# Transposing Q and K on TensorE's row halves, V products on GpSimd, and a new order: causal attention with a gated convolution on one core

## The chip, the core and the metric

The kernel runs on one core of one Trainium2 chip. The core has five engines that run side by side and meet only at semaphores: TensorE (PE: matmuls and transposes, written to the eight PSUM banks), VectorE (DVE), ScalarE (ACT: exponentials, tanh, copies), GpSimd (POOL: no PSUM access) and SyncE (SP: issues transfers). The metric is the device time of one execution in microseconds (us), lower is better.

## The reference

Eight batches, eight heads, 576 positions, head size 64; then a gated linear unit with a causal convolution of five taps over 512 channels.

```python
def _attn_ref(q, k, v, s):
    scores = np.matmul(q, k.transpose(0, 1, 3, 2)) / np.sqrt(D)
    causal = np.triu(np.ones((S, S), dtype=bool), k=1)
    cum = np.cumsum(np.maximum(s, 0.0), axis=-1)
    bias = -(cum[:, :, :, None] - cum[:, :, None, :])
    scores = np.where(causal, -1e9, scores + np.minimum(bias, 0.0))
    attn = np.exp(scores - scores.max(-1, keepdims=True))
    attn = attn / (attn.sum(-1, keepdims=True) + 1e-09)
    return np.matmul(attn, v)

def _moe_ref(x, w_val, conv_w, w_out):      # x: heads side by side, (B, S, 512)
    xp = np.concatenate([np.zeros((B, 4, D)), x], axis=1)
    gate_pre = sum(conv_w[k] * xp[:, k:k + S, :] for k in range(5))
    gate = 1.0 / (1.0 + np.exp(-gate_pre))
    return gate * (x @ w_val) @ w_out
```

Inputs and output are 32-bit floats; the kernel computes its matmuls in bfloat16.

## The kernel before

**Tiling.** Heads are taken in pairs: pair n = 4b + p is heads 2p and 2p + 1 of batch b, 32 pairs in all. For each pair Q and K are cast to bfloat16, transposed on TensorE so that the head size lies on partitions (one head on rows 0 to 63, the other on 64 to 127), and copied to a tile `QKT`. The scores are computed with keys on partitions, in three steps (`s0`, `s1`, `s2`) of 1,024 columns over two PSUM banks; each is followed by an exponential on ScalarE (`e0`, `e1`, `e2`) into a tile `P`. The last 64 by 64 block of four pairs at once is `s4` and `e4`. The decay bias goes into V: `vp` multiplies V (with a column of twos for the row sum) by the exponential `w` of the running sum of s. `av0` and `av` multiply `P` with those products for the two heads, `rec` and `nm` normalise, `xt` transposes the result back to channels, `xe` copies it to `xT`. The taps of the convolution are sums `t1` to `t4` into `gp`: a sum `t2`, `t3` or `t4` is made on VectorE straight from PSUM, or on GpSimd out of a product `p2`, `p3`, `p4` that GpSimd or ScalarE has made before. `th` is the tanh that stands for the sigmoid, `val` the matmul with w_val, `glu` their product, `out` the matmul with w_out, `oe` its copy from PSUM and `st` the store, for row blocks of two batches at a time.

**Loads.** Batch 0 is loaded pair by pair: `ld_q.0.p` and `ld_k.0.p` (128 by 512 floats each), cast by `c_q.0.p` and `c_k.0.p`. From batch 1 on, `ld_q.b` and `ld_k.b` each bring both Q and K of two pairs, and `c_q.b`, `c_k.b` cast 2,048 elements a partition. The last 64 rows of all heads come as `tails` (`ld_t`, two transfers), are transposed by `tt` in 32 bits and copied by `te`.

**Order.** Every engine works off its own list strictly in order. All lists are written out by hand in one string, `ORDER`: each word is a step with its engine (S, T, V, A, G for SyncE, TensorE, VectorE, ScalarE, GpSimd) and, behind it, the PSUM bank or buffer that it uses. `s0.9:T:4:1` is the first score step of pair 9 on TensorE in banks 4 and 5 with tile `P` 1. All loads and stores are issued by SyncE. A step on the list waits for its inputs and for its bank or buffer to come free, and all behind it on that engine wait with it.

**What the change touches.** `qk_T` (L461) makes eight transposes of 128 by 128 for a pair into one bank; `qk_evac` (L467) copies that bank's 1,024 elements a partition to `QKT`, through the helper `copy` (L348), which also makes the casts and the `xe` and `oe` copies. `vprime` (L447) is `vp`, on GpSimd or VectorE as the list says. `mask` (L527, `mk`) sets the scores above the diagonal to zero on GpSimd; a pair without `mk` has them pushed down by two more matmuls instead (`future`, L483). `unread` (L555, `wu`) is a matmul of 512 columns whose result nobody reads. In the trace, L475 is a score matmul, L464 a Q/K transpose, L523 an exponential, L540 attention times V, L562 `xt`, L588 a tap sum on GpSimd, L575 a tap product on GpSimd and L573 one on ScalarE.

The transposes and copies in question:

```python
    def qk_T(e, b, p, *w):
        for c, which in enumerate(w or range(2)):
            for j in range(4):
                pe.transpose(bank16[:, at["qt", b, p, *w][0], c * 512 + j * 128:c * 512 + (j + 1) * 128],
                             qk_src(which, b, p, j if w else 4 * c + j), ident)
```

Of the kernel before, what the change touches and what calls it, by code (L numbers as in the profile page):

```python
# [177 lines left out]
ld_q.0.0:S wu.0:T:0 ld_s:S wu.1:T:7 ld_k.0.0:S wu.2:T:0 wu.3:T:7 ld_k.0.1:S wu.4:T:0 ld_t.0:S wu.5:T:7 wu.6:T:0  # L178
wu.7:T:7 ld_cw:S c_q.0.0:G wu.8:T:0 relu:V ld_q.0.2:S wu.9:T:7 scan:V wu.10:T:0 ld_q.0.1:S wu.11:T:7 wu.12:T:0
wu.13:T:7 ld_q.0.3:S wu.14:T:0 c_k.0.1:A wu.15:T:7 c_k.0.0:V wu.16:T:0 ld_k.0.2:S wu.17:T:7 centre:V wu.18:T:0  # L180
wu.19:T:7 ld_v.0.0:S wu.20:T:2 tt.0:T:0 qt.0.0.q:T:1 qt.0.0.k:T:2 qe.0.0.q:V cwT:T:3 qe.0.0.k:A wu.21:T:7 te.0:V
wu.22:T:6 ld_k.0.3:S s0.0:T:4:0 cwc:V s1.0:T:0 ld_v.0.1:S e0.0:A decT:T:2 qt.0.1.k:T:6 c_q.0.1:V wu.23:T:7 e1.0:A
qe.0.1.k:V mk.0:G qt.0.1.q:T:3 s2.0:T:4 qe.0.1.q:V wu.24:T:6 ld_q.1.0:S:0 e2.0:A wu.25:T:7 c_k.0.2:V c_q.0.3:G
s0.1:T:0:1 c_q.0.2:V qt.0.3.q:T:3 expw:A ld_k.1.0:S:2 s4.0.0:T:4 qe.0.3.q:V qt.0.2.q:T:6 vp.0.0:G e4.0.0:A
qt.0.2.k:T:7 e0.1:A qe.0.2.q:V s1.1:T:2 s4.0.1:T:4 qe.0.2.k:V ld_k.1.1:S wu.26:T:6 e1.1:A c_k.0.3:G av0.0:T:0 s2.1:T:6
e4.0.1:A ld_q.1.1:S s0.2:T:2:0 vp.0.1:V e2.1:A av.0:T s2.2:T:4 rec.0:V e0.2:A av0.1:T:6 ld_v.0.2:S nm.0:V av.1:T
c_q.1.0:G:0 e2.2:A qt.0.3.k:T:2 rec.1:V xt.0:T:3 qe.0.3.k:V mk.2:G qt.1.0:T:0 xe.0:A nm.1:V ld_v.0.3:S s1.2:T:4
qe.1.0:A wu.27:T:1 c_k.1.0:G:1 t1.0:V:0 xt.1:T:2 s0.3:T:6:1 e1.2:A xe.1:V s4.0.3:T:0 c_k.1.1:G t2.0:V ld_t.1:S e0.3:A
s4.0.2:T:4 t1.1:V:1 p2.1:G:0 e4.0.2:A ld_v.1.2:S t3.0:V e4.0.3:A s1.3:T:6 s2.3:T:4 e1.3:A c_q.1.1:G ld_v.1.4:S
qt.1.3:T:0 t4.1:V qt.1.2:T:1 ld_v.1.0:S e2.3:A t4.0:V s0.4:T:6:2 vp.0.2:G ld_v.1.3:S qe.1.2:V e0.4:A qt.1.1:T:3  # L190
ld_v.1.1:S av0.2:T:4 ld_wv:S:0 vp.0.3:G qe.1.3:A t3.1:V av.2:T ld_q.2:S:2 s0.6:T:6:0 rec.2:V e0.6:A nm.2:V t2.1:G
tt.1:T:2 av0.3:T:0 ld_t.2:S qe.1.1:V xt.2:T:4 te.1:A av.3:T xe.2:A mk.6:G s2.4:T:6 ld_k.2:S:1 rec.3:V th.1:A:0
s0.5:T:2:1 nm.3:V p3.2:G:0 e2.4:A t1.2:V:1 ld_wo:S:3 xt.3:T:5 s2.5:T:0 e0.5:A xe.3:V ld_v.2.3:S s1.6:T:6 t3.2:G
t1.3:V:2 ld_v.2.2:S e1.6:A s1.4:T:2 ld_v.2.4:S t2.3:V p4.2:G:1 e2.5:A s1.5:T:6 ld_v.2.0:S t2.2:V ld_v.2.1:S e1.4:A
vp.1.0:G s4.1.3:T:0 t3.3:V ld_k.3:S:4 wu.28:T:4 wu.29:T:4 e4.1.3:A s2.6:T:2 vp.1.1:V wu.30:T:4 e1.5:A t4.2:G av0.4:T:0
av.4:T t4.3:V e2.6:A av0.5:T:6 vp.1.2:V av.5:T th.3:A:1 cast_wv:G s0.7:T:2:1 rec.5:V rec.4:V th.0:A:2 av0.6:T:4 nm.5:V
av.6:T e0.7:A nm.4:V xt.5:T:6 vp.1.3:G ld_q.3:S:0 wu.31:T:7 xe.5:A rec.6:V s1.7:T:2 nm.6:V val.1.0:T:0 e1.7:A
# [544 lines left out]
```

## Time and profile before

| what | value |
|---|---|
| median of 3 runs | 194.74 us (194.48 to 195.73) |
| profiled execution, whole | 193.35 us |
| its span, first to last instruction | 191.6 us |
| mean granted TensorE clock | 0.989 |
| busy TensorE / VectorE / ScalarE / GpSimd | 176.6 / 172.9 / 166.2 / 166.8 us |
| DMA, mean over the span | 211 GB/s, 40.43 MB |

All views come from one execution, recorded by the hardware profiler. Busy time counts an engine while an instruction runs on it. The end of a matmul is modelled, so starts are the safer reading for TensorE. The chain of waits goes back from the last instruction to whatever released each step, and so says on whom the end depended. "Idle before" in a group of instructions is the time that the engine stood still ahead of them, with what ended it. An engine's idle time costs something only where the chain passes through it.

### The profile page before, as it was taken

To read this page: it belongs to the slowest core of one execution; us is meant where nothing else is said; L and a number is where in the kernel's file an instruction comes from. 1 tells how busy PE (TensorE), PEld (TensorE's weight loads), DVE (VectorE), ACT (ScalarE), POOL (GpSimd) and SP (SyncE) were. 2 spreads that over 40 slices of the span, in tenths; PEclk is the share of its full clock that TensorE was granted. 3 is DMA by queue.
4 is the path that set the end of the run, shared out by engine and by line. 5 is a ranking of instruction groups with operands and counts; after the bars stand their busy time and mean duration, and the time that the engine had idled before them with its cause. 6 is when DMAs were issued, how large, how long until landed. Compare 5 with 4: busy or idle time off the path is not lost.

```text
span 191.6 us, 6160 instructions
## 1 busy us (share of the span) xinstructions
PE 176.6 (92%) x2481; PEld 119.3 (62%) x2481; DVE 172.9 (90%) x279; ACT 166.2 (87%) x214; POOL 166.8 (87%) x136
## 2 busy tenths in 40 slices
PE   6999796899998999999997899999999999989991
PEld 2457483578556846677755577675756764757740
DVE  5597999889989799998999999999999899999973
ACT  2179999979999699989899989999999999898930
POOL 6036989998999989999999999999999999998910
PEclk9999999699999999999999999999999999999999
DMA  5998999999999997999999999279550005200515
GB/s 149 269 258 305 255 185 288 317 335 239 238 298 292 192 260 285 307 399 189 194 192 314 363 344 216 107 249 254 139 159 29 29 5 201 76 2 3 221 74 207
DMA packets 62281, 40.43 MB, mean 211 GB/s; under 512 B 47333, under 2 KB 49381, under 8 KB 62250
## 3 DMA queue, kind: packets, MB, share of 16 engines
q1 hardware_dynamic: 62250, 40.01, 76.9%
q8 instruction: 20, 0.33, 0.7%
q14 instruction: 11, 0.09, 0.2%
HBM read 30.57 MB, written 9.44 MB: 209 GB/s over the span
## 4 chain that ended last, share of the span: by engine, by line
PE 33%; DVE 21%; ACT 21%; POOL 10%; issue 9%; DMA 3%; SPq 1%; DVEq 0%; ACTq 0%; POOLq 0%
ACT P L523 9%; PE bank L540 9%; PE bank L623 6%; POOL gp L588 5%; PE bank L475 5%; PE bank L606 5%; DVE gp L586 4%; PE bank L464 3%; DVE xn L549 3%; ACT QKT L348 3%; DVE QKT L348 3%; DVE glu L614 3%; ACT th L598 3%; DMA tail<-in_k_dram 3%; POOL pr L575 2%
## 5 line engine op out<-in xcount | busy, mean ns | idle before, releaser
L523 ACT ACTIVATE P<-bank 128x1024 bf16<-128x1024 f32 x96 | 94.5, 1039 | 4.0 <-PE bank L475 2.4
L588 POOL TENSOR_TENSOR gp<-gp,pr 128x572 f32<-128x572 f32 (+2 forms) x38 | 56.2, 1486 | 3.7 <-ACT pr L573 0.9
L586 DVE SCALAR_TENSOR_TENSOR gp<-bank,cwr,gp 128x574 f32<-128x574 bf16 (+2 forms) x58 | 46.1, 802 | 0.6
L475 PE MATMUL bank<-QKT 64*128 64x128 bf16 (+4 forms) x576 | 38.0, 241 | 5.1 <-ACT P L523 2.8
L606 PE MATMUL bank<-xT,wv 128*128 128x288 bf16 x256 | 36.1, 286 | 2.1 <-DVE xT L348 0.6
L540 PE MATMUL bank<-Vp,P 128*128 128x65 bf16 x960 | 35.9, 194 | 0.7 <-ACT P L523 0.5
L540 PEld LDWEIGHTS <-P 128*128 128x128 bf16 x960 | 33.4, 98 | 4.6 <-issue 2.5
L623 PE MATMUL bank<-wo,glu 128*128 128x512 bf16 x144 | 35.3, 380 | 0.1
L575 POOL TENSOR_TENSOR pr<-xT,cwr 128x572 f32<-128x572 bf16 (+2 forms) x28 | 32.7, 1175 | 1.4 <-DVE xT L348 0.8
L475 PEld LDWEIGHTS <-QKT 64*128 64x128 bf16 x576 | 18.5, 94 | 21.8 <-issue 14.8
L606 PEld LDWEIGHTS <-wv 128*128 128x128 bf16 x256 | 23.8, 97 | 10.7 <-issue 3.4
L448 POOL TENSOR_TENSOR Vp<-vst,w 128x650 bf16<-128x650 f32 x22 | 29.0, 1335 | 0.5 <-ACT w L369 0.5
L598 ACT ACTIVATE th<-gp,cwr 128x576 f32<-128x576 f32 (+1 forms) x33 | 25.2, 780 | 3.1 <-POOL gp L588 1.9
L584 DVE SCALAR_TENSOR_TENSOR gp<-xT,cwr,bank 128x576 f32<-128x576 bf16 x32 | 25.7, 809 | 1.3 <-ACT xT L348 0.2
L549 DVE TENSOR_TENSOR xn<-bank,recs 128x640 bf16<-128x640 f32 x32 | 26.0, 819 | 0.6
L348 ACT COPY QKT<-bank 128x1024 bf16<-128x1024 bf16 (+1 forms) x25 | 24.9, 1014 | 1.8 <-PE bank L464 1.8
L614 DVE SCALAR_TENSOR_TENSOR glu<-th,bank 128x576 bf16<-128x576 f32 (+1 forms) x33 | 23.9, 731 | 2.5 <-ACT th L598 1.1
L529 POOL TENSOR_SCALAR_AFFINE_SELECT P<-P 128x1024 bf16<-128x1024 bf16 x16 | 17.5, 1094 | 8.8 <-ACT P L523 8.8
L623 PEld LDWEIGHTS <-glu 128*128 128x128 bf16 x144 | 12.5, 97 | 14.0 <-issue 2.3
L464 PE MATMUL bank<-ident,qkb 128*128 128x128 bf16 x256 | 19.3, 219 | 0.3 <-DVE gp L586 0.3
L464 PEld LDWEIGHTS <-qkb 128*128 128x128 bf16 x256 | 15.4, 98 | 3.5 <-issue 1.6
L348 POOL CAST qkb<-first 128x2048 bf16<-128x2048 f32 (+2 forms) x11 | 15.5, 1410 | 0.8 <-DMA first<-in_k_dram 0.4
(61 smaller groups left out, 182.7 us busy)
## 6 DMA issues: line engine op xcount, KB each, us to landing
out_dram<-ot SPq DMA_DIRECT2D x36, 256.0 KB, 3.1
...
```

The costliest lines, as they stand in the source:

```text
L348: (act.copy if e is act else e.tensor_copy)(dst, src)
L464: pe.transpose(bank16[:, at["qt", b, p, *w][0], c * 512 + j * 128:c * 512 + (j + 1) * 128], qk_src(which, b, p, j if w else 4 * c + j), ident)
L475: pe.matmul(ps[:, hh, c0:c0 + nq], QKTs[b % 2][r, 1, p, k0:k0 + 128], QKTs[b % 2][r, 0, p, q0:q0 + nq], **kw)
L523: act.activation(out=Pt(n)[:, :, step * 512:(step + 1) * 512], in_=pair((f"s{step}", n)), func=AF.Exp, scale=0.125)
L540: pe.matmul(ps[:, qb * 65:qb * 65 + 65], lhsT, Vps[b % 2][:, kb, 2 * p + hh, :], start=(kb == 0), stop=(kb == qb))
L549: vec.tensor_tensor(xns[b % 2][:, :, p * 128:(p + 1) * 128].rearrange("t g (w d) -> t w g d", w=2), pair(("av", n))[:, :, 0:325].rearrange ...
L575: pool.tensor_tensor(pr, xTs[b % 2][:, c, 4:4 + S - m], r.to_broadcast([128, S - m]), ALU.mult)
L586: vec.scalar_tensor_tensor(gp[:, m:S], xps(n)[:, 0:S - m], r, gp[:, m:S], ALU.mult, ALU.add)
L588: pool.tensor_tensor(gp[:, m:S], gp[:, m:S], prs[at[f"p{m}", n][0]][:, m:S], ALU.add)
L598: act.activation(out=thof(n)[:, r], in_=gps[at["t1", n][0]].rearrange("p (h s) -> p h s", h=2)[:, r], func=AF.Tanh, scale=cwr[:, n % 4, 4:5])
L606: pe.matmul(ps, wv[:, dc, c * 128:(c + 1) * 128], xTs[b % 2][:, dc, 4 + o:4 + o + 288], start=(dc == 0), stop=(dc == 3))
L623: pe.matmul(bank_of(u, i), glu2[:, c, i * 128:i * 128 + 128], wo[:, c, :], start=(c == 0), stop=(c == 3))
```

## The change

Four things change in the code, and the whole order is another one.

1. From batch 1 on (the second batch), a step `qq.b.h` takes the place of two steps `qt`: it transposes two pairs in halves. Each 128 by 128 transpose becomes two of 64 rows by 128 columns, one from TensorE's rows 0 to 63 and one from rows 64 to 127, written to two different banks. Each bank then holds half of both pairs, and `qk_evac` reads both banks for a pair. 28 of the 32 pairs go this way; batch 0 keeps `qt`.
2. All 32 `vp` are on GpSimd (22 before; ten were on VectorE).
3. Loads are issued by the engine that the list names. Six of batch 0's eight Q and K loads go out from ScalarE's queue, the rest stay on SyncE's.
4. `tt` and `te` can use two banks; no step of the new list does.

```diff
-            sync.dma_start(out=first[part][which],
+            e.dma_start(out=first[part][which],
                            in_=(q, k)[which][0, HP[part], 0:512, :].rearrange("h (p j) d -> p h (j d)", j=4))
...
+        if ("qq", b, p // 2) in at:
+            copy(e, QKTs[b % 2][:, :, p, 0:512].rearrange("d w (r x j) -> d w r x j", r=2, j=8),
+                 both_rows(b, p).rearrange("d r (j x w) -> d w r x j", w=2, j=8))
+            return
...
+    def half_T(out, src, r):
+        return pe.transpose(out, src[64 * r:64 * r + 64, :], ident[64 * r:64 * r + 64, 64 * r:64 * r + 64])
+
+    def both_rows(b, p):
+        lo, hi = sorted(at["qq", b, p // 2])
+        return bank16[:, lo:hi + 1:hi - lo, p % 2 * 512:p % 2 * 512 + 512]
+
+    def qk_T2(e, b, h):
+        for p in range(2):
+            for j in range(8):
+                for r in range(2):
+                    half_T(both_rows(b, 2 * h + p)[:, r, j * 64:j * 64 + 64], qk_src(None, b, 2 * h + p, j), r)
```

The list begins like this, before and after (SyncE, ScalarE, GpSimd, VectorE; TensorE without the `wu`):

```diff
-S ld_q.0.0 ld_s ld_k.0.0 ld_k.0.1 ld_t.0 ld_cw ld_q.0.2 ld_q.0.1 ld_q.0.3 ld_k.0.2 ld_v.0.0 ld_k.0.3
+S ld_q.0.0 ld_t.0 ld_q.0.1 ld_s ld_cw ld_v.0.0 ld_v.0.1 ld_k.1.0 ld_k.1.1 ld_q.1.0 ld_v.0.2 ld_q.1.1
-A c_k.0.1 qe.0.0.k e0.0 e1.0 e2.0 expw e4.0.0 e0.1 e1.1 e4.0.1 e2.1
+A ld_k.0.0 ld_k.0.1 ld_k.0.2 ld_q.0.2 ld_k.0.3 ld_q.0.3 c_q.0.0 qe.0.0.k e0.0 e1.0 e2.0 qe.0.2.k e0.1 e1.1 e2.1 expw
-G c_q.0.0 mk.0 c_q.0.3 vp.0.0 c_k.0.3 c_q.1.0 mk.2 c_k.1.0
+G c_k.0.0 c_k.0.1 c_q.0.1 mk.0 c_q.0.2 c_k.0.3 mk.1 vp.0.0 vp.0.1 c_k.1.0 mk.2 c_k.1.1
-V relu scan c_k.0.0 centre qe.0.0.q te.0 cwc c_q.0.1 qe.0.1.k qe.0.1.q
+V qe.0.0.q te.0 qe.0.1.k c_k.0.2 relu qe.0.1.q scan centre qe.0.2.q
-T tt.0 qt.0.0.q qt.0.0.k cwT s0.0 s1.0 decT qt.0.1.k qt.0.1.q s2.0
+T qt.0.0.k qt.0.0.q tt.0 s0.0 qt.0.1.k s1.0 qt.0.1.q s2.0 qt.0.2.k s1.1 s0.1
```

Where the new list has other numbers of steps:

| step | before | after |
|---|---|---|
| Q/K transposes | 36 `qt` | 8 `qt`, 14 `qq` |
| `vp` on GpSimd / VectorE | 22 / 10 | 32 / 0 |
| `mk` on GpSimd | 16 | 19 |
| tap sums `t2` to `t4` on GpSimd / VectorE | 38 / 58 | 35 / 61 |
| tap products on GpSimd / ScalarE | 28 / 10 | 23 / 12 |
| `oe` on ScalarE / VectorE | 20 / 16 | 23 / 13 |
| `xe` on ScalarE / VectorE | 11 / 21 | 9 / 23 |
| `qe` on ScalarE / VectorE | 25 / 11 | 26 / 10 |
| Q/K casts on GpSimd / VectorE / ScalarE | 18 / 5 / 1 | 20 / 2 / 2 |
| `wu` | 33 | 43 |

Of the casts, `c_k.5` (2,048 elements) moves from VectorE to GpSimd and `c_k.2` (2,048 elements) from GpSimd to ScalarE. The count of `wu` up to `av.6` rises by twelve. TensorE's list has 130 places before and 146 after where work on all 128 rows follows work on row halves, or the other way round.

More of the change, by code (lines that the diff above doesn't have):

```diff
@@ L177 @@
 ORDER = """
[L178 to L197, printed above, removed]
```

200 lines of the change are left out of this document (116 added, 84 removed).

## Prediction

> **What bounds the kernel now.** I read the page first: its chain of waits says which engine the end hangs on.
>
> ```profile
> span 191.6 us, 6160 instructions
> ...
> PE 33%; DVE 21%; ACT 21%; POOL 10%; issue 9%; DMA 3%; SPq 1%; DVEq 0%; ACTq 0%; POOLq 0%
> ACT P L523 9%; PE bank L540 9%; PE bank L623 6%; POOL gp L588 5%; PE bank L475 5%; PE bank L606 5%; DVE gp L586 4%; PE bank L464 3%; DVE xn L549 3%; ACT QKT L348 3%; DVE QKT L348 3%; DVE glu L614 3%; ACT th L598 3%; DMA tail<-in_k_dram 3%; POOL pr L575 2%
> ```
>
> No engine owns the chain: it changes hands between four. So I cut the span into stages with the view of busy time by windows (busy us of PE, weight loads, DVE, ACT, POOL; then TensorE's granted clock, DMA share, GB/s).
>
> ```profile
> 0.00:20.00 20.00, 18.17 (x199) 10.54 (x199) 13.79 (x35) 10.95 (x15) 9.05 (x19) 1.00 0.93 250
> 20.00:42.00 22.00, 18.58 (x321) 12.60 (x320) 20.71 (x32) 20.48 (x27) 20.78 (x17) 0.92 1.07 267
> 33.50:38.30 4.80, 4.28 (x65) 2.51 (x65) 4.33 (x5) 4.80 (x7) 4.80 (x4) 0.64 1.12 318
> 42.00:182.00 140.00, 134.30 (x1941) 93.92 (x1939) 133.28 (x205) 133.25 (x171) 136.14 (x102) 1.00 0.74 201
> ```
>
> In the 140 us from 42 on, GpSimd is fullest (136.1) and the others follow within 3 us. The stage is the fullest engine's work plus 3.9 us in which it waits for another. Only before 20 us is there real slack: GpSimd 9.05 of 20, ScalarE 10.95. The last 9.6 us are a tail whose steps the change leaves as they are. So the question is what each engine's load becomes in the two stages, and what the fullest one then waits for.
>
> **The change part by part.** *Transposes on row halves.* This is TensorE's timeline (start, us, line, shapes, count).
>
> ```profile
> 113.27 0.61 PE L464 MATMUL bank<-ident,qkb 128*128 128x128 bf16 x8
> 113.71 0.44 PE L562 MATMUL bank<-ident,xn 128*128 128x128 bf16 x5
> 114.09 0.40 PE L475 MATMUL bank<-QKT 64*128 64x128 bf16 x8
> 114.42 0.63 PE L540 MATMUL bank<-Vp,P 128*128 128x65 bf16 x15
> ```
>
> ```profile
> 102.92 0.29 PE L475 MATMUL bank<-QKT 64*128 64x64 bf16 x8
> 103.04 0.27 PE L486 MATMUL bank<-fut,fut 64*128 64x256 bf16 x2
> ```
>
> Ends are modelled, so I use starts. A pair's eight transposes take 113.71 − 113.27 = 0.44 us, 55 ns each. The trace has no half transpose, but the last-block scores (64 rows, 64 columns, the two halves in turn, two banks) have its shape: eight in 103.04 − 102.92 = 0.12 us, 15 ns each. Sixteen halves replace eight transposes: 16 × 15 = 0.24 us for 0.44, a saving of 0.20 us a pair and, for 28 pairs, 5.6 us. Against it: going from whole-array to half-array work costs time. The five transposes at 113.71 take 0.38 us to the next start, where 5 × 0.055 = 0.28 is due: 0.10 us. The order lists have 130 such switches before and 146 after: +1.6 us. Net −4.0 us of TensorE, of which some −3.4 lies after 42 us (12 of the 14 calls). The other end: halves at 28 ns each (no overlap), 0.45 us a pair, gain 0 and the switches stay, +1.6. I take 15 ns, the row of the same shape.
>
> *The copies behind them* read two banks instead of one. The exponentials already read two banks at 1039 ns for 1,024 elements and the copies of one bank take 1031 (below), so I take no change; the other end is a separate start for each bank, two 512-element copies less one whole, 2 × 0.60 − 1.03 = +0.17 us for each of 28, 24 of them on ScalarE.
>
> *V products.* Ten leave VectorE for GpSimd; GpSimd also gets three masks and two small casts, and gives up five tap products and three tap sums. The groups of GpSimd, then views of single tiles (ns min/median/max, first and last start):
>
> ```profile
> L588 POOL TENSOR_TENSOR gp<-gp,pr 128x572 f32<-128x572 f32 (+2 forms) x38 | 56.2, 1486 | 3.7 <-ACT pr L573 0.9 <-DVE recs L545 0.9 <-DVE gp L586 0.3
> L575 POOL TENSOR_TENSOR pr<-xT,cwr 128x572 f32<-128x572 bf16 (+2 forms) x28 | 32.7, 1175 | 1.4 <-DVE xT L348 0.8 <-ACT xT L348 0.5
> L448 POOL TENSOR_TENSOR Vp<-vst,w 128x650 bf16<-128x650 f32 x22 | 29.0, 1335 | 0.5 <-ACT w L369 0.5
> L529 POOL TENSOR_SCALAR_AFFINE_SELECT P<-P 128x1024 bf16<-128x1024 bf16 x16 | 17.5, 1094 | 8.8 <-ACT P L523 8.8
> ```
>
> ```profile
> L588 POOL TENSOR_TENSOR gp<-gp,pr x38: 1393/1404/2267, 27.6 to 181.4; 128x572 f32<-128x572 f32 x17, 128x573 f32<-128x573 f32 x14, 128x574 f32<-128x574 f32 x7
> L575 POOL TENSOR_TENSOR pr<-xT,cwr x28: 1132/1142/1738, 22.1 to 175.8; 128x572 f32<-128x572 bf16 x14, 128x573 f32<-128x573 bf16 x9, 128x574 f32<-128x574 bf16 x5
> L573 ACT ACTIVATE pr<-bank,cwr x10: 729/745/769, 42.8 to 179.8; 128x573 f32<-128x573 bf16 x5, 128x572 f32<-128x572 bf16 x3, 128x574 f32<-128x574 bf16 x2
> ```
>
> ```profile
> L448 POOL TENSOR_TENSOR Vp<-vst,w x22: 1273/1282/1875, 14.4 to 149.1; 128x650 bf16<-128x650 f32 x22
> L448 DVE TENSOR_TENSOR Vp<-vst,w x10: 824/1221/1908, 16.3 to 142.9; 128x650 bf16<-128x650 f32 x10
> ```
>
> ```profile
> L348 POOL CAST qkb<-first x11: 611/1882/1895, 3.9 to 133.0; 128x2048 bf16<-128x2048 f32 x6, 128x512 bf16<-128x512 f32 x3, 128x1024 bf16<-128x1024 f32 x2
> L348 POOL CAST qkb<-qkf x7: 1037/1888/2491, 20.1 to 109.6; 128x2048 bf16<-128x2048 f32 x5, 128x1024 bf16<-128x1024 f32 x2
> L348 DVE CAST qkb<-first x5: 414/426/1648, 6.3 to 82.8; 128x512 bf16<-128x512 f32 x4, 128x2048 bf16<-128x2048 f32 x1
> L348 ACT CAST qkb<-first x1: 619/619/619, 7.5 to 7.5; 128x512 bf16<-128x512 f32 x1
> ```
>
> The medians are close to the minima and the maxima are far off. What stretches a few is seen where a V product runs on VectorE beside them:
>
> ```profile
> 126.84 3.94 POOL L588 TENSOR_TENSOR gp<-gp,pr 128x572 f32<-128x572 f32 x2
> ```
>
> ```profile
> 128.16 1.37 DVE L448 TENSOR_TENSOR Vp<-vst,w 128x650 bf16<-128x650 f32 x1
> ```
>
> Two tap sums take 3.94 us where 2 × 1.40 is usual, and the product itself takes 1.37 where its shortest is 0.82. Busy time beyond count × median is 56.2 − 38 × 1.404 = 2.8 for the sums, 0.7 for the tap products, 0.8 for GpSimd's own V products, 0.6 for one cast: 4.9 us that should go with the VectorE products and the one long VectorE cast, which also leaves. GpSimd's sum: 10 × 1.28 + 3 × 1.09 + 2 × 0.61 − 5 × 1.14 − 3 × 1.40 = +7.4 us, less 4.9: +2.5. After 42 us it is 7 products, −1 mask, −2 sums, −2 tap products, +2.8, less some 4.3: −1.5, so 136.1 → 134.6; the rest falls before 42, mostly into its idle 11 us. If nothing of the stretching goes, 138.9. VectorE loses 10 × 1.22 = 12.2 us, three output copies and a cast of 1.65, and gains five small steps: after 42 us some −9, to 124.
>
> *ScalarE* takes over work. Its groups:
>
> ```profile
> L348 ACT COPY QKT<-bank 128x1024 bf16<-128x1024 bf16 x24 | 24.3, 1031 | 0.0
> L598 ACT ACTIVATE th<-gp,cwr 128x576 f32<-128x576 f32 x31 | 24.3, 796 | 2.1 <-POOL gp L588 1.9 <-DVE glu L614 0.2
> L348 ACT COPY ot<-bank 128x512 f32<-128x512 f32 x20 | 12.0, 606 | 1.5 <-PE bank L623 1.5
> L348 ACT COPY xT<-bank 128x576 bf16<-128x576 bf16 x11 | 7.1, 650 | 0.6 <-PE bank L562 0.5
> ```
>
> Three more output copies, 1.8; two more tap products, 1.5; one short QKT copy, 0.6; the cast c_k.2 of 2,048 elements (0.619 for 512, and 1.031 − 0.606 = 0.43 for each further 512: 1.9); two x copies less, −1.3. Sum 4.5, less 0.1 overlap for each of five: +4.0. After 42 us: the copies and the cast, less one copy of QKT and one tanh that now come earlier, +1.7, so 133.3 → 135.0. Before 42: +2.3.
>
> *The start.* The chain, then ScalarE's timeline:
>
> ```profile
> 3.76 4.96 DMA tail<-in_k_dram
> 8.86 0.63 PE bank L454 x4
> 9.48 0.45 PE bank L464 x8
> ```
>
> ```profile
> 11.18 2.86 ACT L523 ACTIVATE P<-bank 128x1024 bf16<-128x1024 f32 x3 [0.62 <-PE bank L475]
> ```
>
> The first exponential waits for the tails (issued sixth, landed 8.72), then tail transposes, Q and K transposes and copies: 2.5 us. In the change the tails go out right behind ld_q.0.0, Q and K come before tt.0, and after the tails only tt.0 and s0.0 remain: 0.14 + 0.5 + 0.45 = 1.1 us. But six loads now leave ScalarE's queue at once and share the DMA engines. By the tiles' sizes 1.2 MB were ahead of or in the tails before; now 1.05 MB if the queues share evenly, 1.8 MB if the tails' small rows come last; at the 250 GB/s of the first window that is 8.1 to 11.2. I take 8.9, nearer even sharing: e0.0 at 10.0 instead of 11.18 (9.2 to 12.3). ScalarE's sixth load waits until ld_q.0.0 has landed; behind it stand the table load, c_q.0.0 and qe.0.0.k, all due before the tails. SP's queue now has ld_s behind ld_q.0.1, so scan, decT, expw and with it vp.0.0 come later (after e2.1, about 16 us instead of 14.5), when av0.0 is not yet due.
>
> Then 42 us is reached −1.1 + 2.3 − 1.6 = −0.4 us early, if ScalarE's idle time shrinks by 1.6 us. I count on that for this wait:
>
> ```profile
> 39.49 1.02 ACT L523 ACTIVATE P<-bank 128x1024 bf16<-128x1024 f32 x1 [0.96 <-PE bank L486]
> ```
>
> It follows the stretch 33.5:38.3 in which the clock was 0.64; twelve more unread matmuls (wu) stand there now. Ends: −2 and +1.5.
>
> *Sum.* From 42 us on the loads are ScalarE 135.0, GpSimd 134.6, TensorE 134.3 − 3.4 = 130.9, VectorE 124. Fullest: 135.0 instead of 136.1, −1.1. Of the 3.9 us of waiting I take a third off, since two of the four engines now have 4 to 11 us in hand: −1.3. Together −2.4 (ends: −5.0 with no waiting left, +1.7 with ScalarE's extra work all on the path). With −0.4 from the start: **−2.8 us**, a span of 188.8. The profiled execution took 193.35 in all, 1.75 of it around the span; the three runs' median is 194.74, 1.39 above. I shift it: **191.9 us**.
>
> **The rivals.** *Halves don't overlap as the scores do* (28 ns): TensorE 134.3 + 1.4 = 135.7 becomes the fullest, −0.4, waiting as before, −0.4 at the start: 193.9. Against it stand the 15 ns of the scores; for it, that those come in eights, and a call issues 32 with their weight loads. The Trainium skill, "TensorE: Matmul & The Clock Gate", section "Wait — 56ns, not 53.3ns?", says that start-to-start never drops below about 25 ns however few the columns; by that a call takes 32 × 25 = 0.8 us, and the sum comes out as here. The trace disagrees where the halves alternate. Chance 0.08.
>
> *Banks.* A call holds two of eight banks through both copies, 0.48 + 2 × 1.03 = 2.5 us, where a pair held one for 0.44 + 1.03 = 1.5. A score step needs two neighbouring banks; 0.2 us of delay at each of 14 calls, +2.8, eats the gain: 194.7. The Trainium skill, "TensorEngine Tiling (Array Packing)", Gotcha 1, names that price: row tiles raise PSUM pressure, as they write different banks. No run here shows it yet. Chance 0.14.
>
> *ScalarE becomes the bound.* It gets 4.0 us more work, and if it waits as long as now (1.5 us in 20:42, 6.75 after), all of that is on the path, with 1.1 back at the start: +2.9, 197.6. The kernel turns slower where ScalarE sheds less than 2.9 of those 8.3 us of idle time. For it: its waits were on TensorE and GpSimd alike and both remain near full; against it: TensorE, the larger part, is relieved. Chance 0.23.
>
> **How the numbers follow.** The forecast has 0.55. Within 1% (192.8 to 196.7; about what a measurement tells from no change) lie the first two rivals, 0.22, and 0.05 of the forecast's slow side: 0.27. Faster 0.50, slower 0.23. The forecast's own range is 189.5 to 193.5; with the rivals, 189.5 to 197.8.
>
> **What would show it.** Half transposes: starts some 15 ns apart, 28 pairs in about 6.7 us. GpSimd's maxima of L588 and L448 near their medians. First exponential at 10.0. ScalarE busy for about 135 of the 137 us behind the start. It is wrong if the halves come at 25 ns or more, if 128x1024 QKT copies exceed 1.1 us, if e0.0 starts after 11.2, or if ScalarE idles more than 5 us after 42.

## The result, and the profile after

The changed kernel takes 212.8 us (median of 4 runs, 212.23 to 217.28) against 194.61 us for the kernel before on the same chip: 1.0932 times as long, 95% interval 1.0833 to 1.103. The prediction was 191.9 us, 189.5 to 197.8: the kernel was to become faster and became slower, far outside the range. 18.2 us came in, and the question is from where. Some executions of a kernel, changed or not, take over 1.5% more than its fastest: the medians here are of all executions, the ratios with an interval leave those out, and the profiled executions of e2 and e5 below are of that kind.

The page of the changed kernel: span, busy time by engine, and the engines' shares of the chain of waits.

```profile
span 211.0 us, 6560 instructions
...
PE 178.6 (85%) x2693; PEld 117.4 (56%) x2709; DVE 161.2 (76%) x267; ACT 172.2 (82%) x219; POOL 169.5 (80%) x143
...
PE 41%; DVE 20%; ACT 19%; issue 7%; POOL 6%; DMA 5%; ACTq 0%; DVEq 0%
```

Busy times hardly moved: TensorE +2.0 us, VectorE −11.7, ScalarE +6.0, GpSimd +2.7. The span grew by 19.4. So no engine became the bound; all of them wait more. The groups of instructions say on whom. First the exponentials of the kernel before (busy, mean ns, then the idle time ahead of them and what ended it):

```profile
L523 ACT ACTIVATE P<-bank 128x1024 bf16<-128x1024 f32 x96 | 94.5, 1039 | 4.0 <-PE bank L475 2.4
```

The same group and three others of the changed kernel (its lines are shifted: L540 is the exponential, L618 GpSimd's tap sum, L557 attention times V, L562 the reciprocal, L492 a score matmul):

```profile
L540 ACT ACTIVATE P<-bank 128x1024 bf16<-128x1024 f32 x96 | 94.3, 1037 | 14.2 <-PE bank L492 12.2
L618 POOL TENSOR_TENSOR gp<-gp,pr 128x572 f32<-128x572 f32 (+2 forms) x35 | 49.1, 1406 | 11.4 <-DVE gp L616 9.4
...
L557 PE MATMUL bank<-Vp,P 128*128 128x65 bf16 x960 | 36.7, 197 | 3.9 <-ACT QKT L348 3.3
...
L562 DVE RECIPROCAL recs<-bank 128x10 f32<-128x10 f32 x32 | 6.9, 217 | 16.6 <-PE bank L557 12.2
```

ScalarE waits for scores, VectorE for attention times V, GpSimd for VectorE. It goes round, and the row in which it enters is the third: TensorE's attention times V waits 3.3 us for `ACT QKT L348`, ScalarE's copies of Q and K. In the kernel before that group waits 0.7 us in all, and for no such copy. `av` has nothing to do with those copies but PSUM. The view of busy time by windows shows where it happens (busy us of PE, weight loads, DVE, ACT, POOL; then clock, DMA share, GB/s):

```profile
25.00:42.00 17.00, 11.89 (x188) 8.45 (x188) 9.82 (x15) 9.84 (x14) 10.01 (x9) 0.70 1.10 266
42.00:84.00 42.00, 39.29 (x596) 25.60 (x598) 34.40 (x56) 39.41 (x49) 38.16 (x30) 1.00 0.96 257
84.00:94.00 10.00, 7.09 (x112) 4.73 (x112) 6.20 (x10) 6.81 (x10) 8.90 (x8) 0.83 0.80 213
94.00:126.00 32.00, 28.39 (x515) 19.80 (x516) 28.94 (x45) 30.58 (x39) 28.96 (x22) 1.00 0.99 268
126.00:160.00 34.00, 28.89 (x507) 19.40 (x509) 26.62 (x44) 28.26 (x35) 28.86 (x22) 1.00 0.48 113
```

In 25:42, 84:94 and 126:160 TensorE, VectorE and ScalarE all idle: ScalarE for 16.1 of 61 us. In the two stretches between it idles for 4.0 of 74. These three stretches have one thing in common. Each call `qq` writes two banks, and both copies behind it read both. Of the fourteen calls, nine use neighbouring banks; five don't: `qq.1.1` and `qq.1.0` (7 and 2) at 25 to 35 us, `qq.3.1` (7 and 0) at 85 to 90, `qq.6.1` (1 and 6) at 129 to 135, `qq.7.1` (7 and 2) at 153 to 156.

The first of them, step by step. The list there reads (a gap stands for what bears on other things):

```
qq.1.1:T:7:2 xt.1:T:3 ... t4.0:V qe.1.3:A wu.22:T:4 ... xe.1:V e4.0.2:A qe.1.2:A s0.7:T:4:1
```

ScalarE's timeline of the changed kernel (start, us, line, shapes, count, idle before and its releaser):

```profile
25.66 1.04 ACT L540 ACTIVATE P<-bank 128x1024 bf16<-128x1024 f32 x1
27.40 1.01 ACT L348 COPY QKT<-bank 128x1024 bf16<-128x1024 bf16 x1 [0.70 <-DVE gp L616]
28.31 0.28 ACT L517 ACTIVATE P<-bank 128x128 bf16<-128x128 f32 x1
29.09 1.01 ACT L348 COPY QKT<-bank 128x1024 bf16<-128x1024 bf16 x1 [0.49 <-PE bank L573]
```

TensorE's and VectorE's:

```profile
25.84 0.64 PE L582 MATMUL bank<-ident,qkb 64*128 64x64 bf16 x32
26.41 0.45 PE L579 MATMUL bank<-ident,xn 128*128 128x128 bf16 x5
28.47 0.58 PE L573 MATMUL bank<-ident 128*128 128x512 bf16 x1 [1.60 <-ACT QKT L348]
30.15 0.61 PE L492 MATMUL bank<-QKT 64*128 64x128 bf16 x8 [1.10 <-ACT QKT L348]
```

```profile
26.50 0.81 DVE L616 SCALAR_TENSOR_TENSOR gp<-bank,cwr,gp 128x572 f32<-128x572 bf16 x1
28.45 0.46 DVE L348 COPY xT<-bank 128x576 bf16<-128x576 bf16 x1 [1.13 <-ACT QKT L348]
```

The copy at 27.40 (`qe.1.3`) reads banks 2 and 7. It waited for VectorE's `t4.0`, which ends at 27.31 and reads bank 6. When it was done at 28.41, TensorE's unread matmul `wu.22` could start, which writes bank 4, and VectorE's `xe.1`, which reads bank 3. The copy at 29.09 (`qe.1.2`, banks 2 and 7 again) waited for that `wu.22` in bank 4, and the scores `s0.7` at 30.15 (banks 4 and 5) for the copy. A copy of two banks waits, and is waited for, as if it read all six from 2 to 7. The others look the same. At 85 to 90 us the two copies of banks 7 and 0 stand at 86.22 and 88.40, and `av0.11` in bank 4 waits for the first, `out.0.5` in bank 6 for the second:

```profile
87.29 1.07 PE L557 MATMUL bank<-Vp,P 128*128 128x65 bf16 x30 [1.55 <-ACT QKT L348]
89.46 0.38 PE L653 MATMUL bank<-wo,glu 128*128 128x512 bf16 x1 [1.10 <-ACT QKT L348]
```

At 134.19 the call `qq.6.0` (banks 4 and 5) has waited 1.94 us for the copies of banks 1 and 6.

The waits are in the program, not in the chip: the copy itself takes its usual time, 1.01 us, and in the built program `wu.22` and `xe.1` carry a semaphore wait for `qe.1.3`, `qe.1.2` one for `wu.22`, and `s0.7` one for `qe.1.2`. The Trainium skill, "PSUM — Partial Sum Buffer", section "PSUM bank collisions raise a hardware error", says that two engines must be kept apart by bank, a read against a read too. The program keeps to that: the wait of `qe.1.3` for `t4.0` is one of a read for a read. But it took as touched by a pattern that steps over banks everything between its ends.

### The profile page after: what moved, and what is told of

Its sections match the earlier page's. It is cut to its first block, busy times and chain, and to the rows that moved or that the text cites. A ratio compares the mean times of both kernels' runs of the same rounds, so it can differ in the third digit from the quotient of the medians.

```text
span 211.0 us, 6560 instructions
## 1 busy us (share of the span) xinstructions
PE 178.6 (85%) x2693; PEld 117.4 (56%) x2709; DVE 161.2 (76%) x267; ACT 172.2 (82%) x219; POOL 169.5 (80%) x143
## 4 chain that ended last, share of the span: by engine, by line
PE 41%; DVE 20%; ACT 19%; issue 7%; POOL 6%; DMA 5%; ACTq 0%; DVEq 0%
PE bank L557 10%; PE bank L653 9%; ACT P L540 9%; PE bank L636 7%; PE bank L492 6%; ACT QKT L348 6%; DVE gp L616 6%; DVE gp L614 4%; DMA first<-in_q_dram 4%; POOL qkb L348 3%; PE bank L573 3%; DVE xn L566 2%; PE bank L582 2%; DMA first<-in_k_dram 2%; PE bank L579 2%
## 5 line engine op out<-in xcount | busy, mean ns | idle before, releaser
L540 ACT ACTIVATE P<-bank 128x1024 bf16<-128x1024 f32 x96 | 94.3, 1037 | 14.2 <-PE bank L492 12.2
L618 POOL TENSOR_TENSOR gp<-gp,pr 128x572 f32<-128x572 f32 (+2 forms) x35 | 49.1, 1406 | 11.4 <-DVE gp L616 9.4
L616 DVE SCALAR_TENSOR_TENSOR gp<-bank,cwr,gp 128x574 f32<-128x574 bf16 (+2 forms) x61 | 48.4, 804 | 4.2 <-ACT QKT L348 3.4
L492 PE MATMUL bank<-QKT 64*128 64x128 bf16 (+4 forms) x576 | 39.7, 249 | 7.2 <-ACT P L540 4.2
L448 POOL TENSOR_TENSOR Vp<-vst,w 128x650 bf16<-128x650 f32 x32 | 40.5, 1286 | 1.2 <-ACT w L369 1.2
L557 PE MATMUL bank<-Vp,P 128*128 128x65 bf16 x960 | 36.7, 197 | 3.9 <-ACT QKT L348 3.3
L557 PEld LDWEIGHTS <-P 128*128 128x128 bf16 x960 | 34.1, 100 | 10.4 <-issue 6.6
L636 PE MATMUL bank<-xT,wv 128*128 128x288 bf16 x256 | 36.2, 286 | 1.3 <-ACT P L540 1.0
L492 PEld LDWEIGHTS <-QKT 64*128 64x128 bf16 x576 | 20.6, 98 | 27.3 <-issue 23.0
L348 ACT COPY QKT<-bank 128x1024 bf16<-128x1024 bf16 (+1 forms) x26 | 25.1, 998 | 9.2 <-PE bank L582 3.0
L605 POOL TENSOR_TENSOR pr<-xT,cwr 128x572 f32<-128x572 bf16 (+2 forms) x23 | 26.2, 1147 | 7.8 <-DVE xT L348 6.4
L636 PEld LDWEIGHTS <-wv 128*128 128x128 bf16 x256 | 23.7, 97 | 10.2 <-issue 3.7
L546 POOL TENSOR_SCALAR_AFFINE_SELECT P<-P 128x1024 bf16<-128x1024 bf16 x19 | 21.0, 1109 | 1.2 <-ACT P L540 1.2
L348 POOL CAST qkb<-qkf 128x2048 bf16<-128x2048 f32 (+1 forms) x11 | 19.1, 1736 | 3.0 <-issue 2.8
L562 DVE RECIPROCAL recs<-bank 128x10 f32<-128x10 f32 x32 | 6.9, 217 | 16.6 <-PE bank L557 12.2
L573 PE MATMUL bank<-ident 128*128 128x512 bf16 x43 | 14.3, 446 | 5.5 <-ACT QKT L348 1.6
```

What stands on the lines that cost most here:

```text
L348: (act.copy if e is act else e.tensor_copy)(dst, src)
L448: e.tensor_tensor(Vps[b % 2][:, :, HP[p]], vslot(b)[:, :, HP[p]], w[:, :, b * 8 + 2 * p:b * 8 + 2 * p + 2].unsqueeze(3).to_broadcast([128, ...
L492: pe.matmul(ps[:, hh, c0:c0 + nq], QKTs[b % 2][r, 1, p, k0:k0 + 128], QKTs[b % 2][r, 0, p, q0:q0 + nq], **kw)
L540: act.activation(out=Pt(n)[:, :, step * 512:(step + 1) * 512], in_=pair((f"s{step}", n)), func=AF.Exp, scale=0.125)
L557: pe.matmul(ps[:, qb * 65:qb * 65 + 65], lhsT, Vps[b % 2][:, kb, 2 * p + hh, :], start=(kb == 0), stop=(kb == qb))
L605: pool.tensor_tensor(pr, xTs[b % 2][:, c, 4:4 + S - m], r.to_broadcast([128, S - m]), ALU.mult)
```

## The experiments

**Theory A**: those five calls are the loss, by the banks between. **B**: the new order and its start. **C**: GpSimd with all the V products. **D**: any two banks held through both copies, as the prediction's Banks rival had it. All runs are beside the kernel before on the same chip; lines in the split kernels are seven further down.

*Split the five* (e1). In `qk_evac`, ahead of the strided copy:

```diff
+            lo, hi = sorted(at["qq", b, p // 2])
+            if hi - lo > 1:
+                dst = QKTs[b % 2][:, :, p, 0:512].rearrange("d w (r x j) -> d w r x j", r=2, j=8)
+                for i, j in enumerate((lo, hi)):
+                    copy(e, dst[:, :, i], bank16[:, j, p % 2 * 512:p % 2 * 512 + 512].rearrange(
+                        "d (j x w) -> d w x j", w=2, j=8))
+                return
             copy(e, QKTs[b % 2][:, :, p, 0:512].rearrange("d w (r x j) -> d w r x j", r=2, j=8),
```

> The copies of five of the fourteen calls, those whose two banks are not neighbours (2 and 7, 7 and 2, 7 and 0, 1 and 6, 7 and 2), are made as two copies, one for each bank; all else is the changed kernel. Theory A (a copy that reads two banks with one strided pattern is held, and holds others, for all banks between its lowest and its highest): the losses around those five calls go, some 13 of the 18 us, and the time is 197 to 203 us. Rival B (the new order, with its late start and a lower TensorE clock at 20 to 42 us): the time stays at 209 or more. Rival C (GpSimd with all the V products): 209 or more as well. Rival D (any two banks held through both copies): 209 or more, since the two banks are held as long as before.

Measured: 199.4 us, the kernel before 195.19 (1.0216 by the medians; by the executions that an interval would count, 197.35 and 192.70 on the mean, 1.024). Of 18.2 us, 13.5 to 14.0 went with ten copies cut in two. The same place as above, ScalarE, TensorE, and VectorE's `t4.0`:

```profile
26.16 1.03 ACT L547 ACTIVATE P<-bank 128x1024 bf16<-128x1024 f32 x1
27.06 1.10 ACT L348 COPY QKT<-bank 128x512 bf16<-128x512 bf16 x2
28.00 0.34 ACT L524 ACTIVATE P<-bank 128x128 bf16<-128x128 f32 x1
28.17 1.14 ACT L348 COPY QKT<-bank 128x512 bf16<-128x512 bf16 x2
```

```profile
26.33 0.64 PE L589 MATMUL bank<-ident,qkb 64*128 64x64 bf16 x32
26.91 0.45 PE L586 MATMUL bank<-ident,xn 128*128 128x128 bf16 x5
27.25 0.38 PE L580 MATMUL bank<-ident 128*128 128x512 bf16 x1
27.73 0.29 PE L499 MATMUL bank<-QKT 64*128 64x128 bf16 x4
```

```profile
27.00 0.81 DVE L623 SCALAR_TENSOR_TENSOR gp<-bank,cwr,gp 128x572 f32<-128x572 bf16 x1
```

The copies follow the exponential without a gap and run beside `t4.0`, which they waited for before. `wu.22` comes at 27.25 while they run, and `s0.7` at 27.73, 0.8 us behind `xt.1`; in the changed kernel it was 3.7 us. B, C and D, each of which expected 209 or more, don't hold the bulk.

The two traces also show where the time went. Their lists are the same, and so is the granted clock of 18 to 24 us, 0.72. VectorE's reciprocals of a pair start at (us):

| pair | 0 | 3 | 10 | 13 | 17 | 20 | 23 | 31 |
|---|---|---|---|---|---|---|---|---|
| changed | 22.30 | 40.97 | 79.73 | 99.92 | 130.12 | 147.65 | 161.26 | 194.39 |
| e1 | 22.80 | 34.83 | 73.38 | 90.01 | 119.95 | 135.58 | 146.80 | 179.93 |
| later by | −0.5 | 6.1 | 6.4 | 9.9 | 10.2 | 12.1 | 14.5 | 14.5 |

The changed kernel falls behind by 6.6 us where `qq.1.1` and `qq.1.0` stand, by 3.6 at `qq.3.1`, 1.9 at `qq.6.1` and 2.4 at `qq.7.1`. Between these places the distance moves by 0.3 at most.

*Split all fourteen* (e2; `if True:` in place of `if hi - lo > 1:`).

> The copies of all fourteen calls are made one bank at a time (56 copies of 512 elements instead of 28 of 1,024). Theory A: the nine other calls have neighbouring banks, so nothing is held that isn't read; the time is that of the run with five split calls, or up to 3 us more, for 18 more copies at about 0.17 us each. Rival D: a bank comes free one copy earlier everywhere, and the time falls below that run by 2 us or more.

Measured: 199.31 us, ratio 1.0269 (1.0038 to 1.0501). That is level with e1: no price shows for reading two neighbouring banks at a time in nine calls, nor a gain for a bank freed one copy earlier, for which D expected 2 us or more. The interval, 2.3% either way, would not show a small one. The Trainium skill, "TensorEngine Tiling (Array Packing)", Gotcha 1, warns of PSUM pressure from row tiles; two neighbouring banks a call showed none here that could be measured.

*Whole transposes in the same banks* (e3). The list's `qq` become pairs of `qt`:

```diff
-qq.1.1:T:7:2
+qt.1.2:T:7 qt.1.3:T:2
```

> Each of the fourteen calls transposes its two pairs whole again (128 by 128, eight a pair), the first pair into the first of its two banks and the second pair into the other, at the same places of the order; each copy then reads one bank. Theory A: as the run with five split calls, plus the 0.2 us a pair that the halves save, less ten copies' starts: 198 to 205 us. Rivals B and C: 210 or more. If the halves are worth what their starts 15 ns apart say, this run is 1 to 4 us slower than the one with five split calls.

Measured: 201.04 us, ratio 1.0436 (1.032 to 1.0552). Again the bulk is gone without a strided read. Beside the run with five split, on the same chip, this one is 1.6 us longer by the medians and 3.6 by the executions that the intervals count (200.92 against 197.35); 1 to 4 were expected of the halves. The two traces differ by 2.9 us, and some 1.5 of that are there before the first call, where the lists are the same.

*V products alone* (e4). The kernel before, with `vp.0.1`, `vp.1.1`, `vp.1.2`, `vp.2.0`, `vp.2.1`, `vp.4.0`, `vp.5.2`, `vp.6.1`, `vp.6.2` and `vp.7.2` marked `:G` in place of `:V`.

> The kernel before, with its ten V products of VectorE at GpSimd instead, at the same places of the order; nothing else. GpSimd, the fullest engine, gets ten more products of 1.28 us and loses up to 4.9 us of contention. Theory A says little about it: plus 2 to plus 6 us, 196 to 201. Rival C (V products on GpSimd cost the changed kernel its 18 us): plus 10 us or more, over 204.

Measured: 198.21 us, ratio 1.0309 (1.022 to 1.0399): 3.0 us more than the median beside it (195.19), some 6 by the ratio, where nothing else was planned around them. Either is far from 18.

*Two of the five split* (e5; `if hi - lo > 1 and b == 1:`).

> Only the two calls of the second batch that use banks 7 and 2 have their copies made one bank at a time; the three later calls with banks apart (7 and 0, 1 and 6, 7 and 2 again) read both with one strided pattern. Theory A: the first two calls cost some 8 to 9 us of the 13 that splitting all five took away, the three later ones some 4 to 5, each at its own place (85 to 92, 128 to 135, 153 to 157 us): 203 to 206 us, and the loss against the run with five split calls first appears at the third call. If instead what was lost came from the start of the new order alone and the later stretches only followed, the time is as with all five split, 199.4.

Measured: 207.37 us, ratio 1.0636 (1.0497 to 1.0775). By the ratios the two early calls are worth 5.8 us (1.0932 to 1.0636) and the three late ones the remaining 7.7 to 8.2. The interval, some 2.7 us either way, is wide for that, but the table of reciprocals agrees: 6.6 and 7.9. Expected were 8 to 9 and 4 to 5.

So A holds. What is left is 4.2 us (4.6 by 1.024), and for that a mark helps: the start of pair 3's reciprocals, the last of the first batch. In VectorE's timeline of the run with five split:

```profile
34.83 0.22 DVE L569 RECIPROCAL recs<-bank 128x10 f32<-128x10 f32 x1 [0.27 <-PE bank L564]
```

From there to the end of its span (196.5) it takes 161.7 us; in the kernel before the mark is at 29.5 and the rest takes 162.1. The orders differ, so this comparison is rough. Between kernels with the same list behind the mark it is sharp. All runs, with the granted clock of 18 to 24 us:

| run | median us | ratio (95% interval) | clock 18:24 | mark | from there |
|---|---|---|---|---|---|
| before | 194.6 | | 1.00 | 29.5 | 162.1 |
| changed | 212.8 | 1.0932 (1.0833 to 1.103) | 0.72 | 41.0 | 170.0 |
| e1, five split | 199.4 | 1.0216 (medians; 1.024) | 0.72 | 34.8 | 161.7 |
| e2, all split | 199.3 | 1.0269 (1.0038 to 1.0501) | 0.57 | 36.5 | 162.7 |
| e3, whole transposes | 201.0 | 1.0436 (1.032 to 1.0552) | 0.53 | 36.2 | 163.2 |
| e4, before with V on GpSimd | 198.2 | 1.0309 (1.022 to 1.0399) | 1.00 | 29.3 | 166.2 |
| e5, two split | 207.4 | 1.0636 (1.0497 to 1.0775) | 1.00 | 32.8 | 173.0 |
| e6, e1 with V on VectorE | 210.2 | 1.0893 (medians; 1.079) | 0.72 | 34.4 | 173.6 |
| e7, e1 with V early | 198.1 | 1.0256 (1.0154 to 1.0359) | 1.00 | 34.8 | 161.6 |
| e8, e6 and e7 | 208.9 | 1.0767 (1.0672 to 1.0862) | 1.00 | 36.2 | 171.9 |
| e9, e1 with eight `wu` | 198.3 | 1.0172 (1.0092 to 1.0252) | 0.72 | 33.8 | 162.0 |
| e10, e1 with ScalarE relieved | 198.8 | 1.0186 (1.0096 to 1.0276) | 1.00 | 32.8 | 164.1 |
| e11, e9 and e10 | 201.6 | 1.031 (1.0236 to 1.0384) | 0.51 | 36.1 | 164.2 |
| e12, e1 less 8 V products | 197.1 | 1.0137 (0.9991 to 1.0284) | 1.00 | 32.4 | 161.9 |
| e13, e1 less 7 copies | 197.1 | 1.014 (1.0 to 1.028) | 0.72 | 34.3 | 161.3 |
| e14, e12 and e13 | 196.6 | 1.0084 (1.0016 to 1.0152) | 1.00 | 33.3 | 161.3 |
| e15, e1 with the old start, 15 us | 196.4 | 1.0102 (1.0056 to 1.0147) | 1.00 | 32.4 | 162.0 |
| e16, the same, 19 us | 197.2 | 1.0121 (1.0067 to 1.0174) | 1.00 | 32.9 | 162.4 |

*V products back on VectorE* (e6): e1 with `vp.0.1`, `vp.1.1`, `vp.1.2`, `vp.2.0`, `vp.2.1`, `vp.4.0`, `vp.5.2`, `vp.6.1`, `vp.6.2`, `vp.7.2` marked `:V`.

> Five calls' copies split, and the ten V products that the kernel before has on VectorE are on VectorE again, at their places of the changed order. In the kernel before, moving them to GpSimd cost 3.0 us. If that price holds in the new order: 196 to 197.5. If the new order was made for GpSimd and contention of 4.9 us comes back with them, 199.4 to 203. If the rest of the loss is the start alone, 199 to 200.

None of the three came: it takes 11.9 us more behind the mark. One place, VectorE's timeline, then GpSimd's:

```profile
41.89 2.56 DVE L448 TENSOR_TENSOR Vp<-vst,w 128x650 bf16<-128x650 f32 x1
```

```profile
41.86 1.89 POOL L348 CAST qkb<-qkf 128x2048 bf16<-128x2048 f32 x1
49.56 1.14 POOL L612 TENSOR_TENSOR pr<-xT,cwr 128x572 f32<-128x572 bf16 x1 [5.80 <-DVE xT L348]
```

A product of 0.77 us at its shortest takes 2.56 beside a cast on GpSimd, and then GpSimd stands still for 5.8 us for VectorE's next copy of x (1.2 us at that place in e1). In the new order the products' place is GpSimd; what the move cost in the order before doesn't carry over.

*An earlier V product* (e7). SyncE loads s second instead of fifth; VectorE's list begins with `relu scan centre`; `decT` (bank 3) and `expw` come ahead of `tt.0` and `e0.0`; on GpSimd:

```diff
-c_k.0.0 c_k.0.1 c_q.0.1 mk.0 c_q.0.2 c_k.0.3 mk.1 vp.0.0
+c_k.0.0 c_k.0.1 c_q.0.1 mk.0 vp.0.0 c_q.0.2 c_k.0.3 mk.1
```

> Five calls' copies split, and s is loaded second on SyncE's queue instead of fifth, its scan stands first on VectorE's list, the exponential of the weights stands ahead of the first score exponential, and the first V product behind the first mask. Rest theory (the remaining 4 us are the start: the first V product at 18.8 us instead of 14.5, the first reciprocal 4.9 us late): the first product comes at about 13 us, the first reciprocal 2 us or more earlier, and the time falls by 2 to 4 us to 195.4 to 197.4. Rival (the start is taken up later by engines that idle anyway, and the V products on GpSimd hold the rest): 198.5 to 200.

The first product came at 15.40 us instead of 18.82 (13 expected), the first exponential at 13.24 instead of 10.04, as the tails' load had got behind the one of s, and the mark didn't move, though the clock stayed at 1.00, at which e5, e10, e12 and e14 reach 32.4 to 33.3. So the earlier product alone brings nothing; whether the later exponential took back what it brought, this run can't tell.

*Both edits* (e8).

> The two edits together: five calls' copies split, the weights of V early, and ten V products on VectorE. If start and V products cost on their own: 192 to 195, below or near the kernel before. If they are one loss seen twice: as the better of the two.

The loss of e6 again, behind the mark; neither expectation came.

*Fill TensorE at the start* (e9): four `wu` into bank 2 ahead of `tt.0`, four into bank 0 ahead of `qt.0.1.q`.

> Five calls' copies split, and eight more unread matmuls on TensorE where it idles at 8 to 12 us (four ahead of the tail transposes, four ahead of the second pair's Q transposes). In the run without them TensorE is busy 60% of 8 to 18 us (the kernel before 96%), and its granted clock is 0.66 at 18 to 23 us. Clock theory: with the gap filled the clock stays at 1.00 there, and up to 1.7 us of TensorE's time comes back: 197.5 to 198.5. If the clock is no limit for the end: as without, 199 to 200.

*Relieve ScalarE* (e10): `xe.6`, `oe.0.4`, `oe.0.5`, `oe.0.6`, `xe.14`, `te.5`, `oe.1.7`, `oe.1.8` from `:A` to `:V`.

> Five calls' copies split, and eight copies (two of x, five of the output, one of the tails) that the changed order has on ScalarE go to VectorE at their places, 4.8 us of ScalarE's work between 54 and 131 us. ScalarE theory (with the banks' waits gone ScalarE is the fullest engine from 50 us on, 125.3 of 130 us, with 5.1 us more work than in the kernel before, and that is the loss of 4 us that is left): 2 to 4 us faster, 195.4 to 197.4. Start theory (the loss is made before 50 us): 199 to 200. If VectorE has no room in fact: slower than 200.

*Both* (e11).

> Both edits of the two runs above together. If each works on its own: 194 to 196, level with the kernel before. If the clock is no limit: as the run with ScalarE relieved.

The clock theory failed as put: with the filling the clock at 18 to 24 us was 0.72 as without it, and in e11 0.51. That e9's 198.3 us lie where the theory had them is luck. ScalarE's relief made the stretch behind the mark 2.4 us longer, in e10 and e11 alike; that e10's time is no worse comes from a mark 2 us earlier, before anything differs from e1. The lists of e1, e2, e3, e5, e10, e12, e13 and e14 are the same up to the first call; beside them the mark goes with the clock: 32.4 to 33.3 us at 1.00, 34.3 and 34.8 at 0.72, 36.2 and 36.5 at 0.53 and 0.57.

*Work taken away instead of moved* (e12 to e14). A step marked `N` isn't issued:

```diff
-        does[f](engines[e], *ix)
+        if e != "N":
+            does[f](engines[e], *ix)
```

Left out are `vp.2.0`, `vp.2.1`, `vp.3.1`, `vp.4.0`, `vp.5.2`, `vp.6.1`, `vp.6.2` and `vp.7.2` (e12), the copies of the relief but for `xe.6` (e13), all fifteen (e14).

> Five calls' copies split, and eight of GpSimd's V products of the third batch and later are left out (the batches then use the V products of two batches before, so the attention of those pairs is another), 10.2 us less of GpSimd's work. V theory (what is left of the loss, 4 us, is GpSimd with all the V products, as 3.0 us were in the kernel before): 195 to 196.5. If GpSimd is no longer what sets the pace: 198.5 or more.

> Five calls' copies split, and seven of ScalarE's copies are left out (one of x, five of the output, one of the tails; their readers find what was there before), 4.9 us less of ScalarE's work, with nothing moved to VectorE. ScalarE theory (its 5.1 us more of work are the rest of the loss, and relieving it failed only because VectorE had to take the copies): 195 to 197. If ScalarE doesn't set the pace: 198.5 or more.

> Both: eight V products and seven copies left out. If one engine alone holds the rest, this run is no faster than the better of the two; if GpSimd and ScalarE hold it between them, each filling the other's gaps, it is faster than both: 192 to 195. If the rest is the start, all three stay within 1 us of 199.

The times lie between what the sides expected, but the mark settles it: it differs by up to 2.4 us though none of the work left out stands before it, and the rest takes 161.9, 161.3 and 161.3 us where e1 takes 161.7. In the profiled executions 15 us less work on the two fullest engines is worth 0.4 us. Neither sets the pace behind the mark (what does, no run shows), and what is left of the loss lies ahead of it.

*The old start* (e15, e16). The list of the kernel before up to `s1.1`, or up to `av.1`, then the changed list less what is done:

```diff
-ld_k.0.0:A ld_q.0.0:S ld_k.0.1:A wu.0:T:0 ld_t.0:S wu.1:T:7
+ld_q.0.0:S wu.0:T:0 ld_s:S wu.1:T:7 ld_k.0.0:S wu.2:T:0
...
+vp.0.0:G e4.0.0:A qt.0.2.k:T:7 e0.1:A qe.0.2.q:V s1.1:T:2
```

> Five calls' copies split; the list begins as in the kernel before, up to the second pair's first two score steps (about 15 us), and goes on in the changed order with what is left. In the runs so far with the five split, pair 3's reciprocals (the last of the first batch) start at 32.4 to 36.5 us, the earlier the higher the clock at 18 to 24 us, and from there to the end of the span it takes 161.3 to 162.0 us whatever load GpSimd or ScalarE has; in the kernel before 29.5 and 162.1. Start theory (all that is left of the loss lies before those reciprocals): they come 2 to 4 us earlier, at 30.5 to 32.5, the clock stays at 1.00 at 18 to 24, the rest stays at 161 to 163, and the time is 194.5 to 197. Rival (what is won at the start is waited for later): the rest grows by as much, and the time stays at 198 to 200.

> The same with the old start kept up to the second pair's attention times V (about 19 us; one V product is on VectorE, and three steps have other banks, one another buffer). Start theory: pair 3's reciprocals at 29.5 to 31.5, the rest 161 to 163, the time 193 to 195.5, level with the kernel before or just below. Rival: 198 to 200.

In e16 pair 1's mask comes behind its use, so that pair's attention is another. e15's windows (columns as above):

```profile
8.00:13.00 5.00, 4.98 (x54) 3.28 (x52) 3.24 (x9) 2.64 (x4) 0.96 (x1) 1.00 1.17 299
13.00:18.00 5.00, 3.50 (x46) 1.87 (x46) 3.19 (x6) 4.78 (x8) 4.48 (x6) 1.00 1.00 299
18.00:24.00 6.00, 5.54 (x109) 3.65 (x109) 2.48 (x6) 5.54 (x9) 5.19 (x6) 1.00 0.87 241
```

In e15 the start theory's numbers came: mark at 32.4, clock 1.00, the rest 162.0, 196.43 us. But that this is the old start's doing is not shown. A mark of 32.4 to 33.3 is also what the new start reaches in the executions whose clock stays at 1.00 (e5, e10, e12, e14). And on the same chip e12 to e14, with the new start and without work that the traces price at 0.4 us, have ratios of 1.0084 to 1.014 beside the 1.0102 of e15. Nor does a fuller TensorE alone make that clock: at 8 to 18 us it was busy for 8.11 us in e9, whose clock fell to 0.72, for 8.48 in e15 and 6.26 in e10, which kept 1.00. Keeping the old start 4 us longer brought no more, against what was expected.

The rest of the loss, 1 to 2%, stays open. At a clock of 1.00 it is 2.9 us at the mark, and it comes late: pair 2's reciprocals start at 27.7 us in e12, 27.6 in e15 and 27.4 in the kernel before, pair 3's at 32.4, 32.4 and 29.5. Between the two the new list has the first scores of pair 6, the call `qq.1.0` and a copy behind it, work which the old list has at other places. How much of the 2.9 us is lost there, and how much only moved, no run tells. No version was faster than the kernel before.

## Why the prediction was wrong

**The step that failed** is the one on the copies behind the transposes: "The exponentials already read two banks at 1039 ns for 1,024 elements ... so I take no change". As a duration that is right: the 24 copies of ScalarE take 1033 ns on the mean, the predicted 1031. But the step asked only how long a copy runs, not what stands still while it does. The exponentials' two banks are neighbours; these needn't be. The right question was in the diff, `bank16[:, lo:hi + 1:hi - lo, ...]`, and in the bank numbers of the new list. The Banks rival had the right kind of mechanism and the wrong count: two banks held, 0.2 us at each of 14 calls, 2.8 in all. The runs show nothing that can be measured for nine calls and 13.5 to 14.0 us for five, 1.9 to 3.6 a call by the table of reciprocals, because up to eight banks were claimed. That this is again some 2.8 on the mean, for each and not in all, is chance. My sign for it, QKT copies above 1.1 us, could not have shown it; ScalarE idle for more than 5 us after 42 did, with 12.9 us in 42:160 alone.

**Transposes.** Nearly right in their pace. TensorE's timeline of the changed kernel:

```profile
76.75 0.63 PE L582 MATMUL bank<-ident,qkb 64*128 64x64 bf16 x32
77.35 0.39 PE L492 MATMUL bank<-QKT 64*128 64x64 bf16 x4
```

32 halves take 0.60 us to the next start; the predicted 15 ns each and a switch of 0.10 give 0.58. But here work on row halves follows, so no switch is due, and the call at 25.84 above, with whole-array work behind it, takes 0.57: a half takes 18 to 19 ns rather than 15, and the switch doesn't show behind it. The Trainium skill, "TensorE: Matmul & The Clock Gate", section "Wait — 56ns, not 53.3ns?", has a floor of some 25 ns; by that it would be 0.80, and the trace disagrees. What the halves are worth at the end was overrated: −4.0 us of TensorE's time, and 1.5 us behind the mark (163.2 in e3, 161.7 in e1, one execution each).

**V products.** Right in the mechanism and its size. GpSimd's tap sums and V products of the changed kernel (ns min/median/max):

```profile
L618 POOL TENSOR_TENSOR gp<-gp,pr x35: 1393/1404/1535, 36.8 to 200.9; 128x572 f32<-128x572 f32 x14, 128x573 f32<-128x573 f32 x13, 128x574 f32<-128x574 f32 x8
```

```profile
L448 POOL TENSOR_TENSOR Vp<-vst,w x32: 1277/1284/1317, 18.7 to 170.8; 128x650 bf16<-128x650 f32 x32
```

The maxima fell from 2267 and 1875 to 1535 and 1317, and GpSimd's busy time rose by 2.7 us where +2.5 was worked out. That "the stage is the fullest engine's work plus 3.9 us" was wrong as a rule for gains: e12 took 10.2 us of that work away, and the stretch behind the mark stayed (161.9 us against 161.7).

**ScalarE.** Its busy time rose by 6.0, not 4.0. With the five split it is the fullest engine from 50 to 180 us (125.3 of 130), and the time is near this rival's 197.6; but e13 and e14 show that its work is not what is waited for, so the rival falls with its mechanism.

**The start.** The first exponential came at 10.15 us (10.0 predicted):

```profile
10.15 1.94 ACT L540 ACTIVATE P<-bank 128x1024 bf16<-128x1024 f32 x2 [3.03 <-PE bank L492]
```

The first V product came at 18.7 rather than 16; with it at 15.4, in e7, the mark was the same. The step that failed here is that 42 us would be reached 0.4 us early, the clock's drop at 33.5 to 38.3 filled by the `wu`. In e1 the drop did go from there, but came at 18 to 24 instead. TensorE is busy for 60% of 8 to 18 us there, where it had been for 96%; whether that brings the drop is open (last section).

```profile
8.00:13.00 5.00, 2.96 (x35) 1.76 (x35) 2.51 (x4) 2.16 (x3) 1.65 (x3) 1.00 1.21 272
13.00:18.00 5.00, 3.05 (x41) 1.70 (x39) 4.93 (x7) 4.14 (x5) 2.44 (x4) 1.00 0.93 233
18.00:24.00 6.00, 5.93 (x100) 4.35 (x100) 3.62 (x9) 4.50 (x7) 5.18 (x5) 0.72 1.05 293
...
33.00:38.00 5.00, 4.15 (x69) 2.65 (x70) 4.16 (x8) 4.70 (x8) 5.00 (x5) 1.00 0.92 208
```

An earlier first exponential was taken for an earlier start; the tails came earlier, but the second pair's Q did not (its cast begins at 11.35 us in e1, at 11.53 in the kernel before), and TensorE had little to do until then.

**The sum.** Without the strided copies the stretch behind the mark is shorter by 0.4 us instead of 2.4, and the start longer by some 5 us, or 2.9 where the clock stays at 1.00, instead of shorter by 0.4.
